# A weight fold as 64-row passes in two banks, with the feature-map loads issued later and a new order of TensorE's work

## The chip, the cores and the metric

The kernel runs on one core of a Trainium2 chip. The metric is the device time of one execution in microseconds (us), lower is better. Where several runs exist the median is given with the lowest and highest. The traced execution of each kernel is one of its runs, except for the kernel before, whose trace (149.53 us) is a run of its own. A run more than 1.5% above the fastest of its kernel counts as slow, and the ratios leave it out. In the fences PE is TensorE, PEld its weight loads, DVE VectorE, ACT ScalarE, POOL GpSimd and SP SyncE; a small q behind the name means that the engine only issues something.

## The reference, cut to what matters

```python
x  = A_x                                        # 2048 tokens x 448, bf16
xn = layernorm(x)
q, k, v = heads(xn @ wqkv)                      # 16 heads of 28
pq, pk  = q @ w_phi[h], k @ w_phi[h]            # a 28 x 28 map for each head
phi_q   = concat(softmax(pq), softmax(-pq))     # phi_k the same way
o   = (phi_q @ (phi_k.T @ v)) / (phi_q @ sum(phi_k) + 1e-6)
out = x + merge(o) @ wo + silu(xn @ w1) @ w2    # w1: 448 x 1792, w2: 1792 x 448
```

The kernel never computes q and k themselves. It multiplies the q and k weights by the maps of the heads (below: the map) once ("the fold": 448 rows of weights, 16 heads, q and k), subtracts in each head the last of the 28 columns from the other 27 (a softmax does not change by that), and multiplies the tokens by the result.

## The kernel before

A small scheduler written in Python orders the operations of each engine; a waiting operation waits for semaphores. Four parts matter here.

The loads at the start. Loads without `eng` are issued from SyncE's queue, those with `"act"` from ScalarE's. `chain` fixes the order of operations on one engine.

```python
load(Wp[:], A_w_phi.rearrange("(g hl) d f -> (hl d) g f", g=G), "wphi", eng="act", lat=2500.0)   # the map
# ... constants, masks, 38 warm-up products of TensorE with no use for the result ...
load_x(0, 1)                        # input tile 0
load_x(1, 2)                        # input tile 1
load_x(2, 4)
load(w1_sb[:, 0:2, 0:512], ...)     # first columns of w1
load(w1_sb[:, 2:4, 0:512], ...)
load_w1(512, 1024, "act")           # columns 512 to 1023: two loads, the main one from ScalarE
load_x(4, 8)
# ...
chain("wphi warm_act w1_512 ve0 ve1 ev0a ev0 ev1 ve2 ve3 ev2 silu_table".split())
chain("x8 wT_dma0 wT_dma1 wT_dma2 x12 xnT_dma5 xnT_dma7 wT_dma3 wT_dma4 ... wT_dma7 xnT_dma9 ...".split())
```

The fold. `BDphi` holds 112 x 112 blocks, each with the maps of four heads on its diagonal and zeros elsewhere.

```python
def fold_loads():
    for a in range(8):              # q and k weights, transposed by DMA, 112 rows each
        dma_t(wT_sb[:, a, :], A_wqkv[:, a * KP:a * KP + 128], ...)

def fold_mms(k0, slots):            # two calls, each for 2 x 128 rows of the weights
    for kt, fb in zip((k0, k0 + 1), slots):
        for qk in range(2):
            wps = banks[fb + qk][:, 0:G * KP]...
            mms += [(wps[:, g, :], wT_sb[0:KP, qk * 4 + g, KS[kt]:KS[kt] + 128], BDphi[:, g, :], True, True) for g in range(G)]
    pe_mms(mms, "fold", dur=50.0 * len(mms))
    # ... ScalarE copies each last column; VectorE subtracts it from the other 27 and writes Wqk
```

The blocks. The contraction over 448 is 3.5 times 128, so feed-forward, q, k and v run as pairs of 64-row passes: two products at a time, one in the lower 64 rows of the array and one in the upper, each into its own PSUM bank. In the trace of before the two products of a pair start 3 to 4 ns apart, and pairs with 512 columns step 216 ns. `half(1)` takes the same two banks with the row groups swapped, so it waits for `half(0)`.

The order of TensorE is a list of words, `PLAN`. `aF6@0` and `bF6` are the two halves of feed-forward block 6 in banks 0 and 1; `f` a fold, `ak`, `aq`, `av` the projections, `K` key-value products, `M` their mask, `U7` the numerator and denominator of token tile 7, `W7` its output product with `wo`, `R` and `E` the rest of an output tile, `F9` and `Y1` the second feed-forward product.

The softmax here doesn't subtract the row's maximum and nothing guards it: scores larger than these inputs give would overflow.

## Time and profile before

| | before |
|---|---|
| time, median of 3 runs | 149.83 us (149.39 to 150.99) |
| traced execution: span, clock | 148.2 us, 1.0 |
| TensorE busy | 97%, 93% of the chain that ended last |
| input tile 1 landed | 4.37 us |
| first feed-forward product | 6.81 us |
| first 64-row product | 11.68 us |
| first k product (the fold must be finished) | 34.32 us |
| last product | 145.90 us |

The last four rows are read from the times of TensorE's products in the trace, and I use them below to split each kernel into three segments: **S1** from the start to the first 64-row product (11.68 us), **S2** from there to the first k product (22.64 us), **S3** to the last product (111.58 us).

The first fence is the timeline of the kernel before, over its first microseconds (start, length, engine, source line, operation, operands, count; in brackets the idle time before and what ended it; `ACTq` is ScalarE issuing a DMA). `phT` on the second DMA line is the buffer that `w1` is loaded into.

```profile
0.81 0.41 ACTq L503 DMA_DIRECT2D Wp<-in_A_w_phi_dram  x1
1.06 3.91 PE L528 MATMUL psum<-ones_bf 128*128 128x128 bf16 x38 [1.06 <-POOL epst L496]
1.32 0.45 ACTq L503 DMA_DIRECT2D phT<-in_B_w_dram  x1
4.40 0.63 DVE L602 BATCH_NORM_STATS2 st<-x_sb 128x6 f32<-128x448 bf16 x1 [0.37 <-DMA x_sb<-in_A_x_dram]
5.82 0.44 PE L484 MATMUL psum<-ident,RA 128*128 128x128 bf16 x4 [0.84 <-DVE RA L617]
```

The map is issued first and `w1` behind it, at 1.32 us. The layer norm of tile 1 starts at 4.40, as soon as the tile has landed. TensorE's warm-up products end at 1.06 + 3.91 = 4.97, and it stands idle for 0.84 us before it transposes the first tile.

### The profile page before, as it was taken

The page shows a single profiled execution, that of the slowest core. Times are in us where ns is not written, and L with a number is a line of the kernel's source. Part 1 is how long each engine was busy: PE and PEld are TensorE (multiplying, and loading weights), DVE is VectorE, ACT ScalarE, POOL GpSimd, SP SyncE. Part 2 cuts the span into 40 slices and gives each one's busy share as a digit, 9 for nine tenths or more (in the row PEclk, how much of TensorE's full clock was granted, in tenths as well). Part 3 has the DMA queues.
Part 4 walks back from the last instruction along what each step waited for, and adds up shares of the span by engine and source line. Part 5 has one row for each costly group of instructions (what it writes and reads, how often), then busy time and mean ns, then how long its engine had stood idle before and what let it go on. Part 6 is the DMA issues. An engine that isn't in the chain of part 4 may idle for free.

```text
span 148.2 us, 3656 instructions
## 1 busy us (share of the span) xinstructions
PE 143.6 (97%) x1540; PEld 79.3 (53%) x1540; DVE 90.3 (61%) x189; ACT 70.7 (48%) x88; POOL 71.4 (48%) x82
## 2 busy tenths in 40 slices
PE   7799999999999999999999999999999999999994
PEld 7594444554554556646444444555545655455573
DVE  1878997541499949504995003999477802915284
ACT  4477757357999399979555859400012000000000
POOL 7108566510079999998799900799000800000000
DMA  4999955999500000000089570058788467532325
GB/s 101 370 381 211 298 98 97 189 226 347 140 2 4 0 0 7 4 0 4 0 159 168 102 141 4 0 101 172 151 108 176 86 91 144 150 103 51 60 68 184
DMA packets 44352, 17.42 MB, mean 117 GB/s; under 512 B 36912, under 2 KB 43952, under 8 KB 44336
## 3 DMA queue, kind: packets, MB, share of 16 engines
q1 hardware_dynamic: 41168, 14.99, 47.7%
q10 hardware_dynamic: 3168, 2.20, 4.8%
q8 instruction: 12, 0.20, 0.6%
q14 instruction: 4, 0.03, 0.1%
HBM read 6.56 MB, written 1.84 MB: 57 GB/s over the span
## 4 chain that ended last, share of the span: by engine, by line
PE 93%; DMA 2%; DVE 2%; ACT 0%; issue 0%; SPq 0%
PE psum L469 93%; DMA x_sb<-in_A_x_dram 2%; DVE RA L617 1%; PE psum L484 1%; DVE x_sb L855 1%; DVE st L602 0%; ACT xnT L489 0%; SPq L503 0%; DVE mv L603 0%; DVE rstd L608 0%
## 5 line engine op out<-in xcount | busy, mean ns | idle before, releaser
L469 PE MATMUL psum<-xnT,phT 64*128 64x512 bf16 (+1 forms) x428 | 45.7, 350 | 0.3
L469 PE MATMUL psum<-w_sb,hT 128*128 128x448 bf16 (+1 forms) x238 | 45.2, 342 | 0.0
L737 DVE TENSOR_REDUCE Rec<-Ek_sb 128x32 f32<-128x896 bf16 (+1 forms) x20 | 24.3, 1246 | 26.8 <-ACT Ek_sb L489 19.2
L773 POOL TENSOR_TENSOR RA<-Ek_sb,Rec 128x896 bf16<-128x896 bf16 x16 | 27.0, 1721 | 21.1 <-DVE Rec L738 19.7
L489 ACT ACTIVATE hT<-psum 128x1024 bf16<-128x1024 f32 x28 | 27.2, 1023 | 13.2 <-PE psum L469 13.2
L469 PEld LDWEIGHTS psum<-w_sb,hT 128*128 128x128 bf16 x238 | 22.3, 98 | 18.7 <-issue 1.5
L469 PEld LDWEIGHTS psum<-xnT,phT 64*128 64x128 bf16 (+1 forms) x428 | 20.8, 95 | 21.1 <-PE psum L469 1.7
L489 ACT ACTIVATE Ek_sb<-psum 128x864 bf16<-128x864 f32 x24 | 20.2, 933 | 17.4 <-DVE x_sb L855 16.1
L469 PE MATMUL psum<-Wqk,xnT 64*128 64x432 bf16 x224 | 23.7, 343 | 0.1
L747 POOL TENSOR_TENSOR Ek_sb<-Ek_sb,Rec 128x896 bf16<-128x896 bf16 x8 | 13.4, 1696 | 9.6 <-ACT phT L489 9.6
L469 PEld LDWEIGHTS psum<-Wqk,xnT 64*128 64x128 bf16 x224 | 10.4, 95 | 10.1 <-PE psum L469 0.8
L747 POOL TENSOR_TENSOR phT<-phT,Rec 128x896 bf16<-128x896 bf16 x8 | 13.4, 1698 | 0.0
L469 PE MATMUL psum<-wv,xnT 64*128 64x448 bf16 x112 | 12.7, 349 | 0.0
L602 DVE BATCH_NORM_STATS2 st<-x_sb 128x6 f32<-128x448 bf16 x16 | 9.7, 604 | 3.6 <-DMA x_sb<-in_A_x_dram 3.6
L469 PE MATMUL psum<-wo_sb,vaug 128*128 128x448 bf16 (+1 forms) x51 | 11.0, 341 | 0.0
L833 DVE TENSOR_SCALAR den<-psum 128x16 f32<-128x16 f32 x16 | 2.4, 156 | 13.4 <-PE psum L469 13.4
L840 DVE TENSOR_TENSOR vaug<-psum,rden 128x448 bf16<-128x448 f32 x16 | 9.8, 622 | 0.4
L489 ACT ACTIVATE vaug<-psum 128x896 bf16<-128x896 f32 x8 | 7.4, 937 | 5.1 <-PE psum L469 5.0
L617 DVE TENSOR_SCALAR RA<-x_sb,mv,rstd 128x384 bf16<-128x384 bf16 (+4 forms) x29 | 8.9, 344 | 1.4 <-POOL rstd L613 1.2
L855 DVE TENSOR_TENSOR x_sb<-psum,x_sb 128x448 bf16<-128x448 f32 (+1 forms) x13 | 7.1, 582 | 2.9 <-PE psum L469 2.9
L738 DVE RECIPROCAL Rec<-Rec 128x32 f32<-128x32 f32 (+1 forms) x24 | 8.5, 391 | 0.1
L469 PEld LDWEIGHTS psum<-wv,xnT 64*128 64x128 bf16 x112 | 5.5, 94 | 5.2
(51 smaller groups left out, 106.3 us busy)
## 6 DMA issues: line engine op xcount, KB each, us to landing
out_dram<-x_sb ACTq DMA_DIRECT2D x15, 112.0 KB, 1.8
w_sb<-in_B_w_dram SPq DMA_DIRECT2D x1, 1568.0 KB, 7.5
x_sb<-in_A_x_dram SPq DMA_DIRECT2D x3, 448.0 KB, 6.1
wo_sb<-in_A_wo_dram SPq DMA_DIRECT2D x2, 336.0 KB, 8.7
phT<-in_B_w_dram SPq DMA_DIRECT2D x1, 576.0 KB, 6.3
phT<-in_B_w_dram SPq DMA_DIRECT2D x2, 256.0 KB, 4.6
phT<-in_B_w_dram ACTq DMA_DIRECT2D x1, 384.0 KB, 4.9
wv<-in_A_wqkv_dram SPq DMA_DIRECT2D x1, 336.0 KB, 6.7
```

The costliest lines, as they stand in the source:

```text
L469: r = e.matmul(dst, lhsT, rhs, start=st, stop=sp, skip_group_check=True)
L484: r = e.transpose(dst, src, ident[:])
L489: P.op("act", d_act(n), lambda e: e.activation(dst, src, func, scale=scale), reads=[src], writes=[dst], table=table, name=name, **keys)
L602: P.op("dve", 590, lambda e: e.bn_stats(st6[:, t, :], xs), reads=[xs], writes=[st6[:, t, :]], name=f"bnst{t}", okeys_w=["ln"])
L617: P.op("dve", dur, lambda e: e.tensor_scalar(dst, x_sb[:, t, c0:c1], mv[:, t, 0:1], rstd[:, t:t + 1], ALU.subtract, ALU.mult), reads=[xs, ...
L737: P.op("dve", 50 + 967 * n, lambda e: e.tensor_reduce(R2, E4, AXL.X, ALU.add), reads=[E4], writes=[R2], name="Ssum")
L738: P.op("dve", 135 + 210 * n, lambda e: e.reciprocal(R2, R2), reads=[R2], writes=[R2], name="Rrec")
L747: P.op("pool", 1700, lambda e: e.tensor_tensor(E3, E3, Rk[:, :, None].broadcast_to([128, 32, DH]), ALU.mult), reads=[E3, Rk], writes=[E3], ...
L773: P.op("pool", 1700, lambda e: e.tensor_tensor(dst, Eq, Rq.rearrange("p (c j) -> p c j", c=CC)[:, :, :, None].broadcast_to([128, CC, 4, DH ...
L833: P.op("dve", 190, lambda e: e.tensor_scalar(den[:, uq, :], U3[:, :, DH], EPS_DEN, None, ALU.add), reads=[U3[:, :, DH]], writes=[den[:, uq ...
L840: P.op("dve", 620, lambda e: e.tensor_tensor(o3, U3[:, :, 0:DH], rden[:, uq, :, None].broadcast_to([128, H, DH]), ALU.mult), reads=[U3[:, ...
L855: P.op("dve", d_dve(cs.stop - cs.start), lambda e: e.tensor_tensor(res[:, cs], ob, addend[:, cs], ALU.add), reads=[ob, addend[:, cs]], wri ...
```

## The change

The intent: the fold should run in the same mode as its neighbours (64-row passes in pairs), so that no change of mode is needed (92 to 96 ns each in the trace of before), and on blocks of two heads (56 columns) instead of four (112), so that a product spends less of its work on the zeros of a block. This takes nine transposed loads instead of eight, more masks, and smaller and more subtractions. The map is needed only for the first fold, which starts at 26.38 us before, so its load moves from the head of ScalarE's queue into SyncE's. The order list was made anew.

```diff
@@ order of TensorE (cut to the places that matter below; the whole list is new) @@
-... aF11@6 bF11 f2@24 aF8@0 aF10@6 bF8 bF10 f0@24 aF9@0 aF7@6 bF9 bF7 ak2@4 bk2 ...
+... bF13 aF10@6 aF8@0 f0@2 f3@4 bF8 bF10 f2@2 aF9@0 f1@4 aF7@6 bF9 bF7 ak2@4 bk2 ...
+... U2 W4 U6@3 U3@5 W7 W9 s12 W0@2 R4,7 ... F12@1:2 F12:1 F12:11 U15@0 W12 W1@4 R1,8,13 R12,3 F15@23:6 F15:8 E15
@@ loads @@
-        load(Wp[:], A_w_phi.rearrange("(g hl) d f -> (hl d) g f", g=G), "wphi", eng="act", lat=2500.0)
 ...
         load_x(12, 16)
+        load(Wp[8:8 + KP, 0:3, :], phi[P2:P2 + 3 * KP, :].rearrange("(g p) f -> p g f", g=3), "wphi")
+        load(Wp[8:64, 3, :], phi[D - P2:D, :], "wphi1")
+        load(Wp[64:64 + P2, 3, :], phi[0:P2, :], "wphi2")
+        load(Wp0[0:P2, :], phi[0:P2, :], "wphi3")
@@ fold @@
-            for a in range(8):
-                dma_t(wT_sb[:, a, :], A_wqkv[:, a * KP:a * KP + 128], ...)
+            for i in range(NW):                                   # NW = 9
+                c = max(0, KP * i - 64)
+                dma_t(wT(i), A_wqkv[:, c:c + 128], ...)
-        def fold_mms(k0, slots):
 ...
+        def fold_mms(kt, b):                                      # four calls, 128 rows each
+            for i in range(NW):
+                w = wT(i)[:, KS[kt]:KS[kt] + 128]
+                mms.append((banks[b][:, PW * i:PW * i + PW], w[lo], BD[lo, (i - 1) % G, :] if i else BD0[:], ...))
+                if 0 < i < NW - 1:
+                    mms.append((banks[b + 1][:, PW * (i - 1):PW * i], w[hi], BD[hi, (i - 1) % G, :], ...))
+            pe_mms(mms, "fold", dur=26.0 * NW, mode=64, tiles=(b, b + 1))
 ...                                                               # three subtractions instead of one
@@ order on ScalarE and SyncE @@
-        chain("wphi warm_act w1_512 ve0 ve1 ...".split())
+        chain("warm_act w1_512 ve0 ve1 ...".split())
-        chain("x8 wT_dma0 wT_dma1 wT_dma2 x12 xnT_dma5 xnT_dma7 ... wT_dma7 xnT_dma9 ...
+        chain("x8 wT_dma0 wT_dma1 wT_dma2 x12 wphi wphi1 wphi2 wphi3 xnT_dma5 xnT_dma7 ... wT_dma7 wT_dma8 xnT_dma9 ...
```

## The prediction

> **What bounds the kernel now.** I read the page first, for the busy shares and the chain that ended last.
>
> ```profile
> PE 143.6 (97%) x1540; PEld 79.3 (53%) x1540; DVE 90.3 (61%) x189; ACT 70.7 (48%) x88; POOL 71.4 (48%) x82
> ...
> PE 93%; DMA 2%; DVE 2%; ACT 0%; issue 0%; SPq 0%
> ```
>
> TensorE carries 93% of the chain that ended last, and no other engine more than 2%. A busy TensorE need not be a full one, so I took the start times of the matmuls from the trace and compared each step with that of its own kind in an undisturbed run (a pair of 64-row passes with 512 columns steps every 216 ns). From 9.5 us to the end, all that exceeds these steps is three things: 14 changes between 128-row and 64-row passes at 96 ns each (1.34 us), four pauses of 228 to 232 ns (0.92 us), and about 24 ns around groups of small products. So there is no idle time to fill. The time falls only by what is taken out of TensorE's own stream, or by an earlier start of it. The timeline of TensorE around the weight fold shows the part that the change touches:
>
> ```profile
> 22.81 3.64 PE L469 MATMUL psum<-xnT,phT 64*128 64x512 bf16 x30
> 26.38 0.96 PE L469 MATMUL psum<-BDphi,Y_sb 112*128 112x112 bf16 x16
> 27.27 3.20 PE L469 MATMUL psum<-xnT,phT 64*128 64x512 bf16 x28
> 30.40 0.96 PE L469 MATMUL psum<-BDphi,Y_sb 112*128 112x112 bf16 x16
> 31.29 3.19 PE L469 MATMUL psum<-xnT,phT 64*128 64x512 bf16 x28
> ```
>
> Columns are start, length, engine, operation, operands, count. The last feed-forward matmul of the first line starts at 22.81 + 3.64 - 0.376 (its own length) = 26.07; one step of 216 ns later, at 26.29, the next pair could have started. It starts at 27.27. So one fold call costs 0.98 us of the stream: 0.79 for 16 products at about 49 ns, and two changes of mode at 0.096. The second call by the same sum also costs 0.98. Together: **1.96 us**.
>
> The four pauses are at 12.8, 15.2, 25.0 and 34.7 us. The view of waits has them among these five:
>
> ```profile
> PEld psum L469 <- PE psum L469: 2.5, 5, 0.6
> ```
>
> TensorE waits there for itself: each block runs in two halves, the second half swaps the two banks between the row groups and waits for a signal of the first. Where the order has the second half directly behind the first, the pause shows. The order before does so for feed-forward blocks 3, 4 and 11 and for the k block of tile 2, and that is where the four pauses lie.
>
> [...] 96 ns at every one of the 14 changes, 0 between 64-row blocks in different banks. [...] the trace's nearest case, 58 columns in 64-row pairs, steps 31 ns per pair. [...] the 448 packets of 56 bytes of the map lie between those of the first two input tiles, from 2.2 to 3.0 us.
>
> **The change, part by part.**
> *Fold on TensorE.* The products go from 112 rows in full-array mode to 64-row passes in two banks: per 128 rows of the weights, nine products of the lower half and seven of the upper, 56 columns each, which can run side by side. The closest thing in the trace is the key-value product:
>
> ```profile
> 56.14 0.66 PE L469 MATMUL psum<-vaug,Ek_sb 64*128 64x58 bf16 x32
> 56.64 1.44 PE L469 MATMUL psum<-Wqk,xnT 64*128 64x432 bf16 x14
> ```
>
> 16 pairs in 0.50 us are 31 ns a pair. Nine steps are 0.28 us, four folds 1.12 us. Since the neighbours are 64-row blocks, the four changes of mode go. Removed 1.96, added 1.12: **-0.84 us**, of which 0.38 is the mode changes and 0.46 the products.
> *Order.* I read the new order for halves that directly follow each other: feed-forward 3, v 0, k 2. That is three against four: **-0.23 us**. Mode changes apart from the fold are ten in both. The number of value, output and rest products is the same (the rest passes still pack into eight steps). Key-value groups go from six to five: -0.02.
> *Start.* The load of the map leaves the head of ScalarE's queue, and its 448 small packets leave the way of input tiles 0 and 1. The chain begins with tile 1:
>
> ```profile
> 1.27 3.10 DMA x_sb<-in_A_x_dram
> ```
>
> Those packets took 0.31 us when spread over 16 engines, so up to 0.3 us could be won. But the weight load behind them on the same queue also starts about 0.2 to 0.3 us earlier, and its packets are larger (1 KB, 52 ns each against 11) and compete with tile 1 instead. I enter -0.1 (estimate from these numbers).
> *Vector and scalar work.* Per fold two small reads on ScalarE replace one (0.2 us each), and three subtractions of 54, 432 and 378 elements replace one of 864, for which the row is
>
> ```profile
> L595 DVE TENSOR_TENSOR Wqk<-psum,last 128x864 bf16<-128x864 f32 x4 | 4.0, 1052 | 4.0 <-ACT last L489 4.0
> ```
>
> [...] It lies beside TensorE, unless the first k block must wait for it. Before, the last subtraction ended at 33.80 and k started at 34.33. After, counted from the start of the first fold: the last fold ends at 3.5 us and k follows 2.4 us later, at 5.9; two activations of the blocks in between (0.97 us each) hold up the third fold's reads until about 3.6, then two folds' subtractions need 2.25 us and end at 6.1. So k may wait some **0.0 to 0.4 us**; I enter +0.15.
> *Loads.* Four loads of the map and a ninth transposed load are added to SyncE's queue:
>
> ```profile
> 11.07 0.58 SPq L503 DMA_DIRECT2D x_sb<-in_A_x_dram  x1
> 13.83 3.18 SPq L560 DMA_TRANSPOSE xnT<-RA  x2
> 17.06 6.91 SPq L560 DMA_TRANSPOSE Y_sb<-in_A_wqkv_dram  x5
> 24.01 5.46 SPq L560 DMA_TRANSPOSE xnT<-RA  x4
> ```
>
> The four (about 0.45 us each to issue) fit into the queue's wait from 11.65 to 13.83. The ninth adds 1.26 us: it ends near 25.2 and lands, by the shortest 3.1 us from issue, near 27.1 to 27.4. The first fold comes two half blocks (1.3 us) later in the order, less the pause that is gone: 26.29 + 1.30 - 0.23 = 27.36. That is a dead heat: +0.0 to 0.3, I enter +0.1. GpSimd needs the map only then; its mask product will wait for the load (about 17.5 us) and may hold up the layer norm of tiles 8 and later by up to 2 us. Their transposes wait for SyncE until 24 us anyway, so this is hidden.
> *Sum:* -0.84 - 0.23 - 0.02 - 0.10 + 0.15 + 0.10 = **-0.94 us**, 0.6%.
>
> **Rivals.**
> 1. *The evacuation or the ninth load becomes the wait.* Both come out within a few tenths of a us of TensorE's arrival. Against it: the order was evidently chosen anew with these lengths. If both hit, they give back 0.7 us: about 149.5.
> 2. *The map comes too late.* If GpSimd blocks on it in front of the layer norm, TensorE could stall at tiles 4 to 7 or 8 to 15. For it: the queue was nearly full until 17 us (the last input load, issued at 11.07, took 6.1 us to land). Against: SyncE's own order already delays what follows. It would make 150 to 151.
> 3. *The start gains the full 0.3 us or more* because tile 1 lands sooner; TensorE is full from 9.5 us on, so everything shifts. About 148.5.
> 4. *The new folds are slower than the key-value pairs*, because unpaired products and the jump from 64-row blocks cost more. At 50 ns a step they would be 1.8 us, only the mode changes gain: 149.3.
>
> **Range and chances.** 149.83 - 0.94 = 148.89, which I round to 148.9. The three runs before spread from 149.39 to 150.99, so the median itself may be off by 0.3. With stalls of up to 0.7 us on one side and a better start on the other I take 148.0 to 149.9. Two per cent is 3.0 us; the fold in all is 1.96 us, so even deleting it would not reach that: faster 0.03. Slower by 2% needs a stall of 4 us: 0.01.
>
> **What would show it.** The fold rows should be 64 matmuls of 64 rows x 56 columns in four groups of about 0.28 us start to next block, without 96 ns steps beside them; changes of mode 10 instead of 14; pauses of 230 ns three instead of four; the first k block beginning about 1 us earlier than 34.3. A gap of TensorE before the first fold would show the ninth load as the new bound, a gap before the first k block the subtraction. The end of TensorE's stream should come about 0.9 us earlier, its products otherwise unchanged. The prediction is wrong if a gap of over 0.5 us appears anywhere after 10 us, or if the first feed-forward product starts more than 0.4 us earlier or later than 6.8.

## More of the kernel before

The runs of the result's kernel after and of all experiments, with the runs of before beside them, also list the mean clock that was granted to TensorE (1.0 is full speed) and the span from first to last instruction; the six runs of before in the result list no clock.

Between `U` and `W` of a tile, VectorE normalises, and a transposing DMA on SyncE's queue (`o_sb` to `oT_sb`; the trace names both by one buffer, `vaug`) turns the tile over. `W` can't start before this DMA has landed.

The chain of waits before ends with one unbroken piece of TensorE, 110.69 us long, from the k products to the end (start, length, what):

```profile
35.10 110.69 PE psum L469 x1184
```

So nothing that TensorE waits for shows between 35.10 and 145.79 us.

## The result

| | before | after |
|---|---|---|
| time, median of 6 runs of the same rounds | 149.62 us (149.26 to 150.99) | **151.28 us** (150.73 to 151.77) |
| ratio of fast runs | | 1.010, 95% interval 1.0056 to 1.0144 |
| traced execution: span, clock | 148.2 us, 1.0 | 150.0 us, 0.989 |
| first feed-forward product | 6.81 | 7.28 |
| S1, to the first 64-row product | 11.68 | 13.51 (**+1.83**) |
| S2, to the first k product | 22.64 | 21.73 (**-0.91**) |
| S3, to the last product | 111.58 | 112.44 (**+0.86**) |

A ratio here and below is worked out from fast runs of the same rounds, so it is not quite the ratio of the medians. The change made the kernel 1% slower. That is less than 2%, as the prediction expected, but outside its range of 148.0 to 149.9 us. The three segments sum to +1.78 us, which agrees with the spans (150.0 against 148.2). The middle one, where the fold lies, gained what was hoped for. The other two lost more.

The page of the kernel after; its lines of busy shares, the granted clock in 40 slices of the span (tenths), and the chain by engine:

```profile
span 150.0 us, 3741 instructions
...
PE 144.4 (96%) x1572; PEld 80.6 (54%) x1572; DVE 91.3 (61%) x197; ACT 71.8 (48%) x92; POOL 71.6 (48%) x88
...
PEclk9959999999999999999999999999999999999999
...
PE 89%; DMA 6%; DVE 3%; issue 1%; SPq 0%
```

Two things are new. There is a line of the granted clock at all (the page of before has none), and its third slice is 5: half speed. And DMA carries 6% of the chain instead of 2%.

**The start.** The same timeline as before, of the kernel after:

```profile
1.04 0.48 ACTq L510 DMA_DIRECT2D phT<-in_B_w_dram  x1
1.06 3.66 PE L539 MATMUL psum<-ones_bf 128*128 128x128 bf16 x38 [1.06 <-POOL epst L503]
...
4.97 0.63 DVE L637 BATCH_NORM_STATS2 st<-x_sb 128x6 f32<-128x448 bf16 x1 [1.19 <-DMA x_sb<-in_A_x_dram]
...
6.39 0.43 PE L491 MATMUL psum<-ident,RA 128*128 128x128 bf16 x4 [1.67 <-DVE RA L652]
```

`w1` is now issued at 1.04 instead of 1.32, and input tile 1 lands 0.58 us later: 4.95 instead of 4.37. The packet records show why. Tile 1's packets ran from 2.53 to 3.88 us before, and `w1`'s first packet came at 2.88. After, `w1`'s packets begin at 2.22 and tile 1's run from 3.44 to 4.31; 226 of `w1`'s 384 packets had started before tile 1's first, where in before none had. `w1` itself lands 1.43 us earlier (4.76 against 6.19), for which no product has a use: the first feed-forward product before came at 6.81 and did not wait for it. TensorE's idle time ahead of the transposes doubles, from 0.84 to 1.67 us. Of these 0.83 us the later tile accounts for 0.57 (the transposes start at 6.39 instead of 5.82). The rest is the warm-up, which the change does not touch: its 38 products ended 0.25 us earlier, because 26 of them stepped about 107 ns before the step fell to 56, against 31 in the trace of before.

Stretches of 0.75 us of the kernel after (length; busy time of PE, PEld, DVE, ACT and POOL, with the number of instructions; granted clock; DMA share; GB/s):

```profile
6.75:7.50 0.75, 0.53 (x9) 0.46 (x8) 0.75 (x2) 0.63 (x3) 0.00 (x0) 0.92 0.95 372
7.50:8.25 0.75, 0.75 (x9) 0.60 (x8) 0.72 (x3) 0.75 (x2) 0.00 (x0) 0.50 0.99 363
...
9.75:10.50 0.75, 0.75 (x10) 0.75 (x9) 0.00 (x0) 0.02 (x1) 0.00 (x0) 0.50 1.07 372
10.50:11.25 0.75, 0.75 (x14) 0.75 (x12) 0.00 (x0) 0.73 (x2) 0.00 (x0) 0.81 1.13 407
```

The clock is at half from about 7.38 (0.92 leaves 0.12 us of half speed in the first stretch) to about 10.79 (0.81 leaves 0.29 us in the last): 3.41 us. The trace's own record of the clock has the same stretch, 7.38 to 10.79, and within the span no other values than 1.0 and 0.5. One such stretch in 150.0 us makes a mean clock of 1 - 0.5 x 3.41 / 150.0 = 0.989, which is the figure that nearly every disturbed run lists (three runs of e8 list 0.978, which is two such stretches by the same sum). In the trace 29 steps of TensorE take about 107 ns instead of 56, which is 1.47 us.

**The fold.** TensorE's timeline of the kernel after, around the fold (cut to its main lines; most groups of 56 columns are split by the names of their operands):

```profile
29.17 0.39 PE L476 MATMUL psum<-BD,Y_sb 64*128 64x56 bf16 x16
...
29.63 1.89 PE L476 MATMUL psum<-xnT,phT 64*128 64x512 bf16 x15
31.30 0.42 PE L476 MATMUL psum<-BD,Y_sb 64*128 64x56 bf16 x15
...
32.44 0.37 PE L476 MATMUL psum<-BD,Y_sb 64*128 64x56 bf16 x15
...
35.25 1.69 PE L476 MATMUL psum<-Wqk,xnT 64*128 64x432 bf16 x14
```

Two folds lie back to back from 29.17 to 29.63, so one takes 0.23 us: nine steps of 26 ns. The third takes 0.29 and the fourth 0.26. No step of 96 ns stands beside them.

**The late part.** The chain of waits of the kernel after, from 104 us on:

```profile
104.73 2.50 DMA vaug<-vaug
...
107.28 35.04 PE psum L476 x255
...
143.53 0.46 issue
143.99 2.96 DMA vaug<-vaug
```

The unbroken 110.69 us are gone. TensorE waits for transposes of the attention output at 105.1 us (0.14), 106.7 (0.42) and 146.6 (0.25): ahead of W4, W9 and E15 of the order list, 0.81 us in all.

### The profile page after: what moved, and what is told of

Its sections match the earlier page's. It is cut to its first block, busy times and chain, and to the rows that moved or that the text cites. A ratio compares the mean times of both kernels' runs of the same rounds, so it can differ in the third digit from the quotient of the medians.

```text
span 150.0 us, 3741 instructions
## 1 busy us (share of the span) xinstructions
PE 144.4 (96%) x1572; PEld 80.6 (54%) x1572; DVE 91.3 (61%) x197; ACT 71.8 (48%) x92; POOL 71.6 (48%) x88
## 3 DMA queue, kind: packets, MB, share of 16 engines
HBM read 6.57 MB, written 1.84 MB: 56 GB/s over the span
## 4 chain that ended last, share of the span: by engine, by line
PE 89%; DMA 6%; DVE 3%; issue 1%; SPq 0%
PE psum L476 88%; DMA vaug<-vaug 4%; DMA x_sb<-in_A_x_dram 2%; PE psum L491 1%; DVE RA L652 1%; DVE x_sb L890 1%; DVE st L637 0%; DVE vaug L875 0%; SPq L510 0%; DVE rden L870 0%; DVE den L868 0%; DVE mv L638 0%; DVE rstd L643 0%; SPq L1099 0%
## 5 line engine op out<-in xcount | busy, mean ns | idle before, releaser
L476 PE MATMUL psum<-xnT,phT 64*128 64x512 bf16 (+1 forms) x428 | 46.4, 356 | 0.1
L476 PEld LDWEIGHTS psum<-xnT,phT 64*128 64x128 bf16 (+1 forms) x428 | 22.7, 98 | 19.8 <-PE psum L476 0.6
L646 POOL TENSOR_SCALAR ve<-mv 128x1 f32<-128x1 f32 x12 | 2.7, 225 | 11.8 <-DVE mv L638 11.8
```

Of the source, the lines that this page charges most:

```text
L476: r = e.matmul(dst, lhsT, rhs, start=st, stop=sp, skip_group_check=True)
L646: P.op("pool", 200, lambda e: e.tensor_scalar(ve[:, t:t + 1], mv[:, t, 1:2], EPS_LN, None, ALU.add), reads=[mv[:, t, 1:2]], writes=[ve[:, ...
```

## The experiments

Theories at the outset: **A**, the earlier load of `w1` delays tile 1 and the longer idle time drops the clock (S1); rival **B**, the late map or the ninth transposed load delays the fold; rival **C**, the new fold itself is slow; **D**, the new late order puts three output products too close behind their transposes (S3). The sizes below are from the traced execution of each kernel, the times from six runs of each experiment; before has eleven runs on each of the three chips used. The traced run of e5 counts as slow.

| kernel | tile 1 landed | w1 landed (main load) | first 64-row product (S1) | S2 | S3 | last product |
|---|---|---|---|---|---|---|
| before | 4.37 | 6.19 | 11.68 | 22.64 | 111.58 | 145.90 |
| after | 4.95 | 4.76 | 13.51 | 21.73 | 112.44 | 147.68 |
| e1 after + a load ahead of w1 | 4.15 | 6.00 | 11.45 | 22.28 | 112.02 | 145.75 |
| e2 before + late map alone | 5.32 | 5.14 | 13.93 | 22.65 | 111.58 | 148.16 |
| e3 after + more warm-up | 5.08 | 5.04 | 13.10 | 21.65 | 112.75 | 147.50 |
| e4 after + old late order | 4.78 | 4.58 | 12.09 | 22.01 | 113.44 | 147.54 |
| e5 after + map first | 3.59 | 11.89 | 16.57 | 21.73 | 112.10 | 150.40 |
| e6 e5 + three groups moved | 3.44 | 10.13 | 13.18 | 22.02 | 111.59 | 146.79 |
| e7 after + three groups moved | 5.17 | 4.96 | 12.47 | 21.78 | 111.59 | 145.84 |
| e8 e2 + w1 held back | 3.40 | 11.78 | 16.46 | 22.64 | 111.58 | 150.68 |
| e9 before + w1 in line | 3.72 | 9.01 | 12.13 | 22.76 | 111.58 | 146.47 |
| e10 after + w1 in line | 3.35 | 9.31 | 12.43 | 23.38 | 112.18 | 147.99 |
| e11 e10 + three groups moved | 3.36 | 8.12 | 11.25 | 23.69 | 111.68 | 146.62 |
| e12 early map, w1 in line, groups moved | 3.67 | 8.30 | 11.60 | 21.74 | 111.59 | 144.93 |

### e1: the spacer put back

The changed kernel gets a load with no use in the place where the map stood, in its old shape (448 packets of 56 bytes).

```diff
+        Wx = sb("Wx", [KP, G, DH], BF16)
+        load(Wx[:], A_w_phi.rearrange("(g hl) d f -> (hl d) g f", g=G), "filler", eng="act", lat=2500.0)
-        chain("warm_act w1_512 ve0 ...
+        chain("filler warm_act w1_512 ve0 ...
```

> The changed kernel with one thing added: the old small load of the map (448 packets of 56 bytes, into a tile that nothing reads) stands again at the head of ScalarE's queue, ahead of the weight load w1. Theory A (the moved load let w1 start early, its packets crowd out input tile 1, and the longer idle time of TensorE lets its clock fall back): tile 1 lands near 4.4 us instead of 4.95, the first transpose starts near 5.8 instead of 6.4, and the time falls by 0.6 us where the clock was not lost and by up to 1.8 us where it was: 149.5 to 150.7. Rival B (the start is only noise, or comes from the other new work there): no change, 151.3.

Measured: 150.11 us median (149.34 to 151.33), ratio 1.004 (0.9986 to 1.0094), clock 1.0 in all six runs. S1 is 11.45, shorter than before's. Adding a useless load took 2.06 us off S1, as theory A says. But S2 is 22.28 instead of 21.73: 0.54 us of it, from the start at which the step was due, is a wait in front of the first fold, which the changed kernel did not have (0.38 of it shows as idle time in brackets). TensorE's timeline and then SyncE's of this kernel:

```profile
27.66 0.39 PE L477 MATMUL psum<-BD,Y_sb 64*128 64x56 bf16 x16 [0.38 <-POOL Ek_sb L504]
```

```profile
11.74 3.27 SPq L511 DMA_DIRECT2D Wp<-in_A_w_phi_dram  x4
15.05 2.65 SPq L579 DMA_TRANSPOSE xnT<-RA  x2
...
24.68 1.27 SPq L579 DMA_TRANSPOSE wT<-in_A_wqkv_dram  x1
```

The profile names a memset of GpSimd as what ended the wait. The fold does not read that buffer; it ended at that moment by chance. What the fold does read is the ninth transposed load, issued at 24.68 and landed at 27.52, 0.14 before the fold began. The same 0.13 to 0.14 us lie between this landing and the first fold in e4, e6, e7, e10 and e11. This is rival B: hidden in the changed kernel, where the load landed at 28.76, 0.41 ahead of the fold, only because all of TensorE was late. The queue shows its cause too, and e12 tests it. The four small map loads take 3.27 us to issue, so the transposes behind them start at 15.05, not at 13.83 as before, and everything later moves.

### e2: the late map alone

The kernel before, with only its map load moved to SyncE's queue behind the last input load.

```diff
-        load(Wp[:], A_w_phi.rearrange(...), "wphi", eng="act", lat=2500.0)
 ...
         load_x(12, 16)
+        load(Wp[:], A_w_phi.rearrange(...), "wphi")
-        chain("wphi warm_act w1_512 ve0 ...
+        chain("warm_act w1_512 ve0 ...
-        chain("... x12 xnT_dma5 ...
+        chain("... x12 wphi xnT_dma5 ...
```

> The kernel before with one thing moved: its load of the map is issued after the last input load, as in the change; fold and order stay as before. Theory A: tile 1 lands 0.5 us later, TensorE starts 0.6 us later and in some executions on the slow clock, so 150.2 to 151.4, with none of the savings. Rival B (the late load is harmless): 149.6, as before.

Measured: 151.2 us (149.91 to 151.76), ratio 1.0066 (1.0011 to 1.012); the clock was 0.989 in three of six runs. TensorE's timeline:

```profile
6.76 0.44 PE L484 MATMUL psum<-ident,RA 128*128 128x128 bf16 x4 [1.81 <-DVE RA L617]
```

The idle time ahead of the first transposes is 1.81 us, tile 1 lands at 5.32, 28 steps run at half clock, and S1 is 13.93. S2 and S3 are before's, to 0.01 us. So the whole loss of S1 comes with the moved load alone, with the old fold and the old order. That excludes rival C as its cause.

### e3: the gap filled with more warm-up products

```diff
-        for i in range(38):
-            P.op("pe", 107.0, ...
+        for i in range(68):
+            P.op("pe", 107.0 if i < 38 else 30.0, ...
```

> The changed kernel with 30 more of the dummy products that keep TensorE busy before the first transpose, so that its idle time from 4.7 to 6.4 us is filled. Theory C (the idle time costs the clock, about 1.1 us of the loss): the granted clock is 1.0 in every run, the first 24 feed-forward products step 56 ns and not 107, the time falls by about 1 us to 150.3; tile 1 still lands near 4.95. Rival (the slow steps are not from the idle time): no change, 151.3.

Measured: 149.83 us (149.4 to 151.04), ratio 1.0003 (0.9955 to 1.0051), clock 1.0 in five runs and 0.999 in one. The clock stayed up with TensorE kept busy, and this alone takes the changed kernel from 1.010 to the level of before, in spite of the late tile. The traced run was its slowest (151.04): 62 of the dummies ran before the first transpose, took 6.45 us, and put it off to 7.34, and two late waits (0.75 and 0.39 us) remained. So this is a remedy for the clock, not for the tile.

### e4: the old late order on the new head

From `bq8` on, the order list of before.

```diff
-... bq8 K6-8 bq0 aF17@4 K8-10 bF17 ...  F12@1:2 F12:1 F12:11 U15@0 W12 W1@4 R1,8,13 R12,3 F15@23:6 F15:8 E15
+... bq8 aF17@4 K6-10 bq0 aF14@2 bF17 ...  F11:1 F11:1 W11 W1@4 F12:9 W12 U15 W13 W14 R14,12 R13,11 R1,2 F15@07:5 F15:5 F15:4 E15
```

> The changed kernel with its order up to the second q block and the order of the kernel before from there on. Theory D (the new order puts output products too close behind the transposes that they wait for): the waits of 0.14, 0.42 and 0.25 us at 105, 107 and 147 us go away and the time falls by about 0.8 us to 150.5. Rival (the waits come from a general delay of the transposes): they show elsewhere, 151.3.

Measured: 151.31 us (150.56 to 151.63), ratio 1.0086 (1.0041 to 1.0131), clock 1.0 in all six. A miss: S3 grew to 113.44. The chain of waits has

```profile
134.59 4.56 DMA vaug<-vaug
```

a transpose that took 4.56 us, where the same one took 2.42 in before (whose sixteen range up to 5.06, with a median of 2.6), and TensorE waited 1.39 us for it. The old order is thus free of late waits only behind its own head. Why that transpose was slow stays open. It also shows that full clock in all runs does not by itself make a run short.

### e5, e6, e7: map first, and three groups moved

e5 puts the four map loads first on ScalarE's queue, ahead of the activation and `w1`. For this the two memsets that clear the map's tiles also move ahead, and the first warm-up product starts at 1.24 us instead of 1.06. e7 leaves the loads as changed, and moves three groups of the late order so that the transposes get more time. e6 has both.

```diff
 e7 and e6:
-U2 W4 U6@3 U3@5 W7 W9 s12 W0@2 R4,7
+U2 W7 U6@3 U3@5 W4 s12 W0@2 W9 R4,7
-F12@1:2 F12:1 F12:11 U15@0 W12
+F12@1:2 F12:1 U15@0 F12:11 W12
 e5 and e6:
-        load(Wp[8:8 + KP, 0:3, :], ..., "wphi")       # and wphi1 to wphi3, on SyncE
+        load(Wp[8:8 + KP, 0:3, :], ..., "wphi", eng="act", lat=2500.0)     # all four, ahead of everything
-        chain("warm_act w1_512 ve0 ...
+        chain("wphi wphi1 wphi2 wphi3 warm_act w1_512 ve0 ...
```

> The changed kernel with its four loads of the map put back to the head of ScalarE's queue (w1 behind them), fold and order as in the change: what the change is without the later load. The first run of this study with the old small load as a mere filler gave 150.1, with tile 1 at 4.15 us, but a wait of 0.54 us before the first fold, for the map's mask product. Theory A: here tile 1 lands by 4.4 and that wait goes or shrinks to what the ninth transposed load costs (under 0.3), so 149.4 to 149.9. Rival (four issues delay w1 too far): the third feed-forward product waits for w1 after 9 us, 150.5 or more.

> As the run before it, and three groups moved in the late order: the output products of tiles 4 and 9 behind those of 7 and 0, and the attention product of tile 15 ahead of 11 feed-forward products. Theory D (the waits of 0.14, 0.42 and 0.25 to 0.39 us are for transposes issued too shortly before): they go, 0.8 us less than the run before it, 148.6 to 149.1, faster than the kernel before by 0.5%. Rival E (the queue of transposes is full, so a wait taken away comes back at the next product): no change against the run before it.

> The changed kernel with only those three groups moved. Theory D: 0.8 us less than the changed kernel, 150.5, with the start as bad as there (tile 1 near 4.95, granted clock 0.989 in most runs). Rival E: 151.3.

(Where the texts for e5 and e6 speak of a wait for the mask product of the map, they follow the misleading releaser of e1; the wait was for the ninth load.)

On this chip the kernel before had the clock at 0.989 in 5 of 11 runs, so its median is 151.21 and the intervals are wide: e5 151.05 (ratio 1.0012, 0.9948 to 1.0075), e6 150.4 (0.9957, 0.9886 to 1.0028), e7 149.94 (0.9947, 0.9876 to 1.0018). The ratio of e7 also leaves out one of its two runs with a lost clock, because it counts as slow. In runs at full clock, before's mean is 150.11 (6 runs), e6's 150.05 (6), e7's 149.51 (4).

The traces do tell the theories apart. *e7*: tile 1 still lands late (5.17), the clock happens to stay up in the traced run, and S3 is 111.59. Its chain of waits ends again with

```profile
35.04 110.69 PE psum L476 x1184
```

the very length of before. S3 goes from 112.10 to 111.59 in e6 against e5, too. Theory D holds for the three groups: the loss of S3 came from their place in the order. *e5 and e6*: tile 1 lands at 3.59 and 3.44, which confirms A from the other side, but now `w1` is late (issued at 3.12, landed at 11.89 and 10.13), the third feed-forward product waits 3.2 us for it in e5 and 0.4 us in e6, where 1.1 us went before to a load of the first `w1` columns that landed at 9.00. In the trace of e5 the gap is followed by a stretch at half clock; that run was slow (154.05 us), the five others of e5 list a clock of 1.0, and I draw nothing from its total. Both missed the times expected of them; for e5 the rival came true (a wait for `w1`, 150.5 us or more).

### e8: w1 held back by another means

e2, with `w1` behind the first small activation on ScalarE instead of ahead of it.

```diff
-        chain("warm_act w1_512 ve0 ve1 ...
+        chain("warm_act ve0 w1_512 ve1 ...
```

> The kernel before with the map loaded late, as in the second run of this study (151.2, tile 1 at 5.32), but with the issue of w1 on ScalarE's queue held back behind the first layer-norm instruction, at about 4 us. Theory A (it is w1's early packets that hold up tile 1, not the absence of the small ones): tile 1 lands by 4.2, clock 1.0, 149.6 or a little less. Rival (the late map itself costs the time, in the fold or the layer norm): about 151.

Measured: 154.82 us (152.15 to 156.03), ratio 1.0183 (1.0091 to 1.0275), clock 0.978 to 1.0; three of the six runs count as slow, and the ratio is that of the other three. A miss as a remedy, useful as a test. Tile 1 lands at 3.40, and the first feed-forward product starts at 6.03. TensorE's timeline then shows the price:

```profile
11.83 0.84 PE L469 MATMUL psum<-xnT,phT 128*128 128x128 bf16 x12 [3.49 <-DMA phT<-in_B_w_dram]
```

The first product that needs these columns waits 3.49 us, and after it 32 steps run at half clock. So `w1` must come early enough for the products at 8 us, and late enough to let tile 1 pass.

### e9, e10, e11: w1 in line with the input tiles

`w1` moves to SyncE's queue, behind the first `w1` columns, so that it can no longer overtake tile 1 (e9 on before, e10 on after, e11 is e10 with the three groups moved).

```diff
-        load_w1(512, 1024, "act")
+        load_w1(512, 1024)
-        chain("... warm_act w1_512 ve0 ...
+        chain("... warm_act ve0 ...
```

> The kernel before with the weight load w1 (the second group of columns) issued on SyncE's queue, in line behind the first group, instead of on ScalarE's at the start; the map's load stays at the head there. If w1's early packets are what holds up tile 1, tile 1 lands near 3.5 us instead of 4.37, w1 still lands before 8 us, in time for the third feed-forward product, and the first feed-forward product starts 0.4 to 0.8 us earlier: 149.0 against 149.7 of the kernel before with a clock of 1.0. Rival (the packets then only crowd another load that the start needs): no change.

> The changed kernel with that one move of w1, the map still loaded late. Theory A: tile 1 near 3.5 us, no cold clock (1.0 in all runs), and a wait before the first fold of 0.5 to 1.2 us for the map's mask product or the ninth transposed load, late waits as in the changed kernel: 149.6 to 150.2, against 151.3. Rival (the start isn't what costs): 151.3.

> As the run before it, with the three groups moved in the late order. Theory D: 0.8 us less, 148.8 to 149.4, and no wait of TensorE over 0.1 us after 36 us. Rival E: no change against the run before it.

Measured: e9 150.37 us (149.65 to 151.35), ratio 1.0051 (1.0001 to 1.01). e10 150.8 (149.39 to 151.58), 1.0071 (1.0019 to 1.0123). e11 150.35 (149.64 to 151.17), 1.0046 (0.9998 to 1.0095). All three missed the times expected of them. The clock was 1.0 in all 18 runs. Tile 1 lands at 3.35 to 3.72. In e9 and e10 `w1` now comes a little too late (9.01 and 9.31): e10 waits 1.3 us for it, and e9 0.4, after 0.5 for a load of the first columns that landed at 7.96. In e11, with the same loads, it lands at 8.12, so this date itself varies by over 1 us from run to run. Rival B is plain in e10 and e11: the ninth load lands at 29.60 and 28.74, and the first fold waits 1.06 and 1.66 us for it, since TensorE now arrives in time and SyncE's queue has grown by another load. TensorE's timeline of e11 names the load:

```profile
28.87 0.39 PE L476 MATMUL psum<-BD,Y_sb 64*128 64x56 bf16 x16 [1.48 <-DMA wT<-in_A_wqkv_dram]
```

Another 0.6 us (e10) and 0.3 us (e11) of S2 go to a wait of a feed-forward product at 22.1 and 20.6 us, in e10 for a transposed input tile. Moving the three groups again takes S3 from 112.18 to 111.68.

### e12: all of it together

`w1` in line as in e10, the four map loads on ScalarE's queue, behind its first activation in the order (the trace has them issued from 1.22 to 3.16), with no `w1` behind them, and the three groups moved.

```diff
-        chain("warm_act w1_512 ve0 ve1 ...
+        chain("warm_act wphi wphi1 wphi2 wphi3 ve0 ve1 ...
-        chain("... x12 wphi wphi1 wphi2 wphi3 xnT_dma5 ...
+        chain("... x12 xnT_dma5 ...
         # and the edits of e7 and e10
```

> As the run before it, with the four loads of the map early on ScalarE's queue, where w1 stood. The wait for the mask product before the first fold goes, and what the ninth transposed load costs stays (0.3 to 0.8 us, more the earlier TensorE is): 148.3 to 148.9. Rival: the four loads' 504 small packets cost the start as much as they save later, no change against the run before it.

Measured: **148.93 us** (148.53 to 149.21), against 149.59 (149.15 to 151.65) for before on the same chip; ratio 0.9954 (0.991 to 0.9998). The clock was 1.0 in all six runs; before had 0.989 in two of eleven. It is faster than before by little more than the interval allows; there is no run of the changed kernel in the same rounds, whose median was 151.28. The page and the chain of waits:

```profile
span 147.3 us, 3741 instructions
```

```profile
3.72 5.11 DMA phT<-in_B_w_dram
...
34.13 110.69 PE psum L476 x1184
```

There is no wait before the fold (the ninth load lands at 26.83, the fold starts at 27.27) and none after 35 us:

```profile
27.27 0.39 PE L476 MATMUL psum<-BD,Y_sb 64*128 64x56 bf16 x16
```

The expectation still reckoned with 0.3 to 0.8 us for the ninth load. Against e11, which differs only in where the four map loads and the two memsets of their tiles stand, the ninth load lands 1.91 us earlier and S2 is 1.95 us shorter. So it was the four small loads on SyncE's queue that made the fold wait, and not the ninth load itself. The chain still starts with `w1`, whose second, smaller load lands at 3.72 + 5.11 = 8.83: this is what limits S1 now. S1 is 11.60 (-0.08 against before), S2 21.74 (-0.90), S3 111.59 (+0.01), in sum -0.97 us at the last product.

## Why the prediction was wrong

Its sum was -0.94 us; the traces gave +1.78. By its own steps:

- **What bounds the kernel: right.** TensorE's stream is the bound, and each loss was a stretch in which that stream stood still or ran at half clock.
- **Fold on TensorE: right, too small.** Predicted -0.84. Four folds measured 0.23 + 0.23 + 0.29 + 0.26 = 1.02 us in place of 1.96: -0.94. The step is 26 ns in the first two, not 31. In the key-value row an ordinary pair steps 29 ns, and every eighth, whose weights have 112 columns, 51; the fold has none of the latter. Why 29 there and 26 here is not shown. Rival 4 (and C) is refuted by these rows and by S2.
- **Order: right.** Three pauses (14.6, 20.5 and 35.6 us) instead of four, ten changes of mode instead of fourteen (the latter are part of the fold's 0.94): -0.23.
- **Wait of the first k block: right.** Predicted +0.15; the last subtraction ended at 35.10 and k waited 0.17. The three subtractions of a fold took 1.10 us from start to start, so 2.20 for two folds, against 2.25 predicted; that figure was the author's estimate, which the row that it shows, 1.05 us for one subtraction, does not give by itself. A second small wait of 0.19, for the bank that ScalarE empties behind the fold, was not predicted. Together -0.94 - 0.23 + 0.17 + 0.19 = -0.81, and S2 measured -0.91; the other 0.10 us are not accounted for.
- **Loads: too small, and hidden by luck.** Predicted +0.1, from a landing of the ninth load at 27.1 to 27.4 us and a fold at 27.36. It landed at 28.76. The changed kernel has no such wait because it arrives at the fold 1.8 us late; with the start mended, as in e1, e10 and e11, the wait is 0.5 to 1.7 us. The prediction put the issue of the four map loads at 0.45 us each; in e1 they took 3.27 / 4 = 0.82 each, and e12 shows that without them on this queue the ninth load lands at 26.83, in time. Rival 1 of the prediction had named this wait.
- **Start, "I enter -0.1": the step that failed.** It weighed two effects, 0.3 us won by the missing small packets against a loss to the larger packets of `w1`, and guessed the balance. The sign was wrong: tile 1 landed 0.58 us later. Runs whose first loads differ by one load give the two sizes. Without `w1` in the way, tile 1 lands at 3.72 with the map's packets (e9) and at 3.35 without them (e10): 0.37 us won, close to the 0.3. But `w1` delays tile 1 by 4.37 - 3.72 = 0.65 us where the map is ahead of it (before), and by 4.95 - 3.35 = 1.60 us where it is not (after): 0.95 us lost, where the prediction had entered about 0.2. (These are single traces; with the head of after, tile 1 landed between 4.78 and 5.17 in e3, e4 and e7.) And it had no term for the 3.41 us at half clock that followed the longer idle time of TensorE. Together S1 lost 1.83 us. That it was the load's place, and neither fold nor order, is shown by e2 (which reproduces it alone) and e1 (which undoes it). The half clock is shown in the trace; e3 keeps it away by filling the gap.
- **"Its products otherwise unchanged": the second step that failed.** The prediction assumed that a new late order has no new waits. It has three, 0.81 us of the 0.86 that S3 lost, and e7, e6 and e11 remove them by moving three groups.

The text named the sign that would prove it wrong, a first feed-forward product more than 0.4 us off 6.8 us. It came at 7.28. With both failed steps mended (e12), the last product comes 0.97 us earlier than before, almost all of it in S2, where the fold lies. That this is so near the predicted 0.94 is partly luck: a larger gain at the fold stands against the unforeseen wait of 0.19. So the mechanism of the fold was right, and the cost of moving a load was not.

**What stays open.** The split in three is that of one traced execution for each kernel. The changed kernel's two runs near full clock (150.73 and 151.77) were no shorter than its four at 0.989 (mean 151.30), so in them other waits must have taken the place of the half clock; only their spans are kept. The same kernel varies by 1 to 2 us between runs at full clock (e10 149.39 to 151.58), which I did not trace. Also open are the 0.46 us before the last transpose is issued in the changed kernel, and the slow transpose of e4.

## What to carry to other kernels

A load that seems useless early may be a spacer: before you move it, ask which load behind it on the queue will start earlier, and whose packets that one will get in front of (here 226 of 384 packets, and a tile 0.58 us later). Early in a kernel count the idle time of TensorE as a risk to its clock, not only as idle time (here 1.67 us of it, and then 3.41 us at half clock), and compare the clock of several runs. When part of the change is a new order, look for the shortest distance between each transposing DMA and its reader, because a sum over instructions has no term for it (here 0.81 us of waits).

## What the traces show of the clock, the loads and the mode

- The clock: in the traced runs one stretch of 3.41 us at half clock followed 1.67 us (after) and 1.81 us (e2) of idle TensorE ahead of eight transposes, and none followed 0.84 (before) or 1.31 (e7); up to the first feed-forward product behind the transposes the idle and transposing time is 2.56, 2.71, 1.84 and 2.20 us. It differs from run to run: 4 of 6 runs of after, 3 of 6 of e2, 2 of 6 of e7, 8 of the 33 of before whose clock is listed, none of the 6 of e12. In after the record of the clock begins at 3.96 us with 3.41 us at 1.0, in which the whole gap lies (4.72 to 6.39), and the stretch at half clock comes next; before 3.96 it has no entry, and there the warm-up products stepped 107 ns. In e7 all 38 warm-up products took 4.24 us, which is 107 ns a step up to the gap. What decides whether the clock falls is not shown.
- The start of a load: one issued 0.28 us earlier from the other queue, with nothing ahead of it, went with a tile that landed 0.58 us later (after against before), and with it out of the way the tile landed 0.65 us (e9 against before) to 1.60 us (e10 against after) sooner.
- The issue of small loads from SyncE: four of 3 to 18 KB took 3.27 us in e1, and 1.91 us for the same four in the changed kernel.
- A change of mode: 92 to 96 ns for each of the 14 of before and the 10 of after.
- Pairs of 64-row products: one with 56 columns stepped 26 ns (after, first two folds).
